# A bucketed attention and expert kernel: denominators of the last pair by one-column products, route and gather steps in the order list, a new order

## The chip, the cores and the metric

The program runs on one core of one Trainium2 chip. The metric is the device time of one execution in microseconds. The kernel before took 443.05 us (median of three runs, 442.56 to 443.46).

## The reference

Attention in which a query sees only the keys of its own hash bucket (six signs of a projection), and then a mixture of eight experts, of which each token goes to one:

```python
mask = q_bucket[:, :, :, None] == k_bucket[:, :, None, :]
scores = scale * np.matmul(q, k.transpose(0, 1, 3, 2))
scores = np.where(mask, scores, -1000000000.0)
attn = np.exp(scores - np.max(scores, axis=-1, keepdims=True))
attn = attn / (np.sum(attn, axis=-1, keepdims=True) + 1e-09)
x = np.matmul(attn, v)                       # B, H, S, D = 2, 8, 768, 64
...
# x as [B, S, 512]; per batch, in the order of the tokens s:
e = fresh_e if s == 0 or local_gate[b, s] < 0.5 else prev_e   # fresh_e = argmax(logits)
h = np.maximum(x[b, s] @ w1[e], 0.0)         # w1: 8, 512, 1024
out[b, s] = p[e] * (h @ w2[e])               # w2: 8, 1024, 512
```

All inputs and outputs are fp32.

## The kernel before

The 16 heads are worked as eight pairs, p = 0 to 7 (four to a batch); the two heads of a pair lie side by side on the partitions or the columns of TensorE. Queries and keys are cut in six tiles of 128 and two halves of 384. Per pair:

- `s1(p, i, kh)`: scores of query tile i against half kh of the keys, two terms (rounded values; bucket bits), and their row maximum on VectorE (line 262).
- `s2(p, kt, half)`: transposed scores of key tile kt against half of the queries, four terms, and the exponential on ScalarE (line 309) into a `pt` tile, of which there are ten.
- `padd(p, kt, h)`: the sums of the `pt` tiles, kept as `SP[p, h]` (line 316), on VectorE or GpSimd as `MOVED` says. `pv` multiplies `pt` by V (line 323), `flat` adds the uniform rows (line 330).
- `hp`, `hd`, `bd`: bucket bits of the next pair; `hi`, `lo`: its split in a rounded value and a rest, on ScalarE, VectorE or GpSimd; `ma`, `mb`, `mc`, `mf`: maxima, transposed and sent by DMA. `lx` loads q and k of a pair.
- `sa`, `sb`: the denominators of a pair, by a product of a ones matrix with `SP`, a copy on ScalarE, and transposes back. The last pair has its own `sah`, `sbh`, by halves: there `SP` holds the sum of the first five (half 0) or four (half 1) `pt` tiles, and further products with ones add the rest (lines 342 to 363).
- `ot`, `ug`: copy of the output, transposes with the gate's product (line 417), normalization into the token rows `XT` and the logits `GR` (lines 425, 430).

`route(b, halves)` is a generator that chooses the expert and the slot of each token and scatters the rows to DRAM `xs` (line 555). It runs on VectorE, with transposes on TensorE, and stops at each `yield`; `step()` runs it to the next one. There are three: batch 0, and the two halves of batch 1. The first expert's tokens of batch 1 don't take the way through DRAM: they are gathered by products with one-hot matrices (`onehot`, lines 635 and 712) on top of the batch 0 rows that `xa` read back (line 751). `we`, `wh`, `wl` and `ve` load and split the first expert's weights. `ready` splits the gathered rows, and `hidden(0, ...)` begins the experts (line 735). `busy` are idle products at the start.

The order of all of it, up to the last `ugh`, is the list `ORDER`: each word is a step, issued in this order to every engine's and queue's own in-order stream. `MOVED` chooses the engine or the queue of a step (0 or 1). Score buffers, and all others in PSUM of the tag `big`, are three of two banks each. After the list some steps stand in the code (gather, `late` normalization, last route steps).

Of the kernel before, what the change touches and what calls it, by code (L numbers as in the profile page):

```python
# [6 lines left out]
F32 = mybir.dt.float32  # L7
F32R = mybir.dt.float32r
# [52 lines left out]
padd.5.4.0 padd.6.1.0 s2.6.2.0 s2.6.3.1 s1.7.1.0 s1.7.1.1 pv.5.4.1 pv.5.5.1 padd.5.5.1 padd.5.5.0 pv.5.5.0 s1.7.2.0
s1.7.2.1 ot.5 s1.7.3.0 mf.6 we.0 we.1 we.2 we.3 pv.6.0.1 pv.6.0.0 s2.6.1.1 s1.7.3.1 s2.6.3.0 s2.6.2.1 lo.7.1 padd.6.1.1 s1.7.4.0 s2.6.4.1
step s2.6.4.0 s2.6.5.1 wh.0 wh.1 s1.7.4.1 padd.6.2.1 pv.6.1.1 pv.6.1.0 s1.7.5.0 padd.6.2.0 s1.7.5.1 sa.5 pv.6.2.1 pv.6.3.1
pv.6.2.0 padd.6.3.0 pv.6.4.1 pv.6.3.0 ma.7 flat.6.0 mb.7 sb.5 ug.4 ug.5 mc.7 step padd.6.3.1 split_h.0 flat.6.1
s2.7.2.0 s2.6.5.0 split_h.1 pv.6.5.1 padd.6.4.0 pv.6.4.0 pv.6.5.0 ot.6 padd.6.4.1 padd.6.5.1 wl.0 wl.1 s2.7.1.0 s2.7.0.0
s2.7.5.0 s2.7.3.0 s2.7.1.1 padd.6.5.0 s2.7.4.0 step padd.7.1.0 mf.7 we.4 we.5 ve.0 ve.1 ve.2 ve.3 split_l.0 s2.7.0.1 sa.6 padd.7.2.0 pv.7.0.0 padd.7.3.0
pv.7.1.0 padd.7.4.0 split_l.1 step wh.2 wh.3 wh.4 pv.7.2.0 sb.6 ug.6 wh.5 wl.2 wl.3 wl.4 wl.5 flat.7.0 padd.7.1.1 sah.7.0 pv.7.3.0 pv.7.4.0 pv.7.5.0 sbh.7.0
oth.7.0 ugh.7.0 s2.7.2.1 s2.7.3.1 step pv.7.0.1 padd.7.2.1 flat.7.1 xa.0 step s2.7.5.1 split_h.2 s2.7.4.1 padd.7.3.1
pv.7.1.1 pv.7.2.1 xa.1 step step hle.0 pv.7.3.1 hle.1 ohe pv.7.4.1 sah.7.1 pv.7.5.1 oth.7.1 sbh.7.1 ugh.7.1
step  # L70
# [7 lines left out]
    "padd": {(0, 3, 1): 1, (1, 1, 0): 1, (1, 1, 1): 1, (1, 2, 0): 1, (1, 2, 1): 1, (1, 3, 1): 1, (1, 5, 1): 1, (2, 1, 1): 1, (2, 2, 0): 1, (2, 2, 1): 1, (2, 5, 0): 1, (2, 5, 1): 1, (3, 5, 0): 1, (4, 1, 1): 1, (4, 2, 1): 1, (4, 3, 0): 1, (4, 4, 0): 1, (5, 1, 0): 1, (5, 2, 0): 1, (6, 1, 0): 1, (6, 1, 1): 1, (6, 2, 1): 1, (6, 5, 0): 1, (7, 1, 0): 1, (7, 1, 1): 1, (7, 2, 0): 1, (7, 2, 1): 1, (7, 3, 0): 1, (7, 3, 1): 1, (7, 4, 0): 1},  # L78
    "split_l": {(2,): 1, (3,): 1},
    "wl": {(2,): 1, (3,): 1, (4,): 1, (5,): 1},  # L80
}

# [44 lines left out]
def tile_kernel(ctx, tc, qT, kT, v, proj, wg, w1, w2, cst, out):  # L127
# [210 lines left out]
    def sah(p, half):  # L338
        st = ps.tile([128, 2, 512], F32, tag="big", name="st")
        ST[p, half] = st  # L340
        for h in range(2):
            nc.tensor.matmul(out=st[32 * h:32 * h + 32, 0, 0:384], lhsT=ones, start=True, stop=False,
                             rhs=SP[p, half][:, h * 384:h * 384 + 384], tile_position=(0, 32 * h))
        for kt in range(5 - half, 6):
            for h in range(2):
                nc.tensor.matmul(out=st[32 * h:32 * h + 32, 0, 0:384], lhsT=ones, start=False, stop=(kt == 5),
                                 rhs=PT[p, kt, half][:, h * 384:h * 384 + 384], tile_position=(0, 32 * h))
        ss = smp.tile([64, 384], F32, tag="ss", name="ss", bufs=1)
        nc.scalar.activation(out=ss, in_=st[0:64, 0, 0:384], func=ACTF.Copy)
        NF[p] = ss  # L350
# [594 lines left out]
```

## Time and profile before

| | us |
|---|---|
| median of three runs | 443.05 |
| the profiled execution, its own time | 442.57 |
| its span, first to last instruction | 440.8 |
| TensorE busy in the span | 424.1 |
| VectorE busy | 285.5 |
| ScalarE busy | 211.2 |
| GpSimd busy | 171.8 |

TensorE's busy time counts pipelined products, whose ends are modelled, so products overlap in it; the distances between their starts tell what each costs. The granted clock of TensorE was 0.995 of full speed over the span. In the views below PE is TensorE, PEld its weight load, DVE VectorE, ACT ScalarE, POOL GpSimd and SP the queue of SyncE; a line number is one of the kernel before.

### The profile page before, as it was taken

Reading aid. Unit: us, or ns where it says so; the run is one execution under the profiler, and the core shown is the slowest. Engines: PE = TensorE matmul, PEld = TensorE weight load, DVE = VectorE, ACT = ScalarE, POOL = GpSimd, SP = SyncE. Lnnn points to the kernel's source line nnn. Section 1 sums busy time; section 2 is a strip of 40 time slices with the busy share of each in tenths; the row PEclk is TensorE's granted clock in tenths of the full one; section 3 lists DMA queues with packets and bytes.
Section 4 is the critical chain, followed back from the end, with each engine's and each line's share of the span. In section 5 each row is a group of like instructions: output and inputs, shape, how many; then the busy total and the mean of one; then the engine's idle time right before and its main releaser. Section 6 shows DMA issues by size and latency. Waiting matters only on the chain.

```text
span 440.8 us, 8126 instructions
## 1 busy us (share of the span) xinstructions
PE 424.1 (96%) x3208; PEld 327.0 (74%) x3208; DVE 285.5 (65%) x453; ACT 211.2 (48%) x290; POOL 171.8 (39%) x124
## 2 busy tenths in 40 slices
PE   8899999999999999999999899999999999999993
PEld 6655575847667566766665898989898989898993
DVE  6766887678466677686988775967565646474110
ACT  3534372716536345362744255757564646463110
POOL 6595545546878636959153121010000000000001
PEclk9999999999999999999999999999999999999998
DMA  7212341224062100310353199997767676750000
GB/s 269 93 41 78 74 141 45 68 76 133 26 217 103 37 13 6 110 38 2 97 193 114 20 268 369 337 328 263 259 201 272 194 268 216 245 165 2 38 2 32
DMA packets 42612, 60.08 MB, mean 136 GB/s; under 512 B 5431, under 2 KB 25129, under 8 KB 42572
## 3 DMA queue, kind: packets, MB, share of 16 engines
q1 hardware_dynamic: 39081, 50.15, 35.5%
q0 software_dynamic: 2432, 6.84, 4.2%
q10 hardware_dynamic: 1059, 2.56, 1.7%
q8 instruction: 26, 0.43, 0.4%
q14 instruction: 14, 0.11, 0.1%
HBM read 47.75 MB, written 11.56 MB: 135 GB/s over the span
## 4 chain that ended last, share of the span: by engine, by line
issue 41%; PE 39%; POOL 6%; DVE 6%; DMA 4%; ACT 0%; POOLq 0%; SPq 0%; DVEq 0%
PE s L253 21%; PE pv L323 13%; POOL out L855 4%; PE ug L417 2%; DVE mx L262 2%; POOL xs L555 2%; DVE sp L316 2%; DMA xk<-kT 2%; PE st L375 1%; DMA xq<-qT 1%; PE pv L330 1%; DVE rE L514 1%; DMA xs<-xt,rsi 1%; PE hb L192 1%; DMA xa<-xs 1%
## 5 line engine op out<-in xcount | busy, mean ns | idle before, releaser
L262 DVE TENSOR_REDUCE mx<-s 128x2 f32<-128x768 f32 x96 | 88.8, 954 | 33.6 <-PE s L253 32.8
L309 ACT ACTIVATE pt<-s 128x768 f32<-128x768 f32 x96 | 74.7, 810 | 47.9 <-PE s L253 46.3
L802 DVE TENSOR_TENSOR wl<-st,wh 128x1024 fp32r<-128x1024 f32 x56 | 67.1, 1221 | 46.7 <-ACT wh L801 46.2
L316 POOL TENSOR_TENSOR sp<-sp,pt 128x768 f32<-128x768 f32 x40 | 75.0, 1887 | 44.4 <-DVE sp L316 35.3
L253 PE MATMUL s<-hx 64*128 64x384 f32 x384 | 72.7, 374 | 2.8 <-DVE mx L262 2.5
L801 ACT ACTIVATE wh<-st 128x1024 fp32r<-128x1024 f32 x56 | 58.3, 1057 | 26.2 <-DMA st<-w 13.3
L323 PE MATMUL pv<-pt,v 128*64 128x384 f32 x384 | 69.9, 496 | 0.0
L855 POOL DMA_INDIRECT out<-y,xsl x13 | 13.2, 1013 | 140.2 <-ACT y L848 140.2
L253 PE MATMUL s<-b,b 64*128 64x384 f32 x372 | 63.0, 334 | 0.0
L253 PEld LDWEIGHTS s<-hx 64*128 64x128 f32 x384 | 36.0, 183 | 27.9 <-DVE mx L262 7.7
L735 PE MATMUL hps<-xH,wh 128*128 128x256 f32 x224 | 53.8, 276 | 0.0
L735 PE MATMUL hps<-xH,wl 128*128 128x256 f32 x224 | 53.7, 277 | 0.0
L845 PE MATMUL yps<-wh,hH 128*128 128x512 f32 (+1 forms) x136 | 52.2, 383 | 0.0
L845 PE MATMUL yps<-wh,hL 128*128 128x512 f32 (+1 forms) x136 | 51.6, 380 | 0.0
L845 PE MATMUL yps<-wl,hH 128*128 128x512 f32 (+1 forms) x136 | 51.4, 378 | 0.0
L323 PEld LDWEIGHTS pv<-pt,v 128*64 128x64 f32 x384 | 24.4, 136 | 31.9 <-issue 31.0
L735 PEld LDWEIGHTS hps<-xH,wl 128*128 128x128 f32 x224 | 42.1, 188 | 0.3
L735 PEld LDWEIGHTS hps<-xH,wh 128*128 128x128 f32 x224 | 42.1, 188 | 0.3
L738 DVE SCALAR_TENSOR_TENSOR hL<-hps,hH 128x512 fp32r<-128x512 f32 x32 | 22.0, 686 | 22.2 <-ACT hH L737 22.2
L253 PEld LDWEIGHTS s<-b,b 64*128 64x128 f32 x372 | 35.1, 184 | 0.0
L735 PE MATMUL hps<-xL,wh 128*128 128x256 f32 x224 | 34.5, 276 | 0.0
L253 PE MATMUL s<-hx,lx 64*128 64x384 f32 x192 | 32.5, 333 | 0.0
(211 smaller groups left out, 631.5 us busy)
## 6 DMA issues: line engine op xcount, KB each, us to landing
st<-w SPq DMA_DIRECT2D x56, 512.0 KB
xs<-z SPq DMA_DIRECT2D x8, 513.0 KB
st<-w SPq DMA_DIRECT2D x13, 256.0 KB
xsl<-xs SPq DMA_DIRECT2D x6, 514.0 KB
v<-v SPq DMA_DIRECT2D x12, 256.0 KB
xq<-qT SPq DMA_DIRECT2D x6, 384.0 KB
xk<-kT ACTq DMA_DIRECT2D x4, 384.0 KB
xk<-kT SPq DMA_DIRECT2D x4, 384.0 KB
```

The costliest lines, as they stand in the source:

```text
L253: nc.tensor.matmul(out=sc[:, h, 0:384], lhsT=w[r, cols[0]], rhs=x[r, cols[1]], tile_position=(64 * h, 0), start=first and n == 0, stop=las ...
L262: nc.vector.tensor_reduce(out=MX[p][:, kh, i // 3, :, i % 3], in_=sc[:, :, 0:384], axis=AX.X, op=ALU.max)
L309: nc.scalar.activation(out=pt.rearrange("p (a q) -> p a q", a=2), in_=sc[:, :, 0:384], func=ACTF.Exp, scale=0.125)
L316: eng.tensor_tensor(out=SP[p, h], in0=PT[p, 0, h] if kt == 1 else SP[p, h], in1=PT[p, kt, h], op=ALU.add)
L323: nc.tensor.matmul(out=PV[p][64 * h:64 * h + 64, half, 0:384], lhsT=V[b, kt][:, pp * 128 + 64 * h:pp * 128 + 64 * h + 64], rhs=PT[p, kt, h ...
L417: nc.tensor.matmul(out=t[:, half, j * 146:j * 146 + 146], lhsT=OT[p][:, q * 128:q * 128 + 128], rhs=iw[:, pp])
L735: nc.tensor.matmul(out=hps[:, k], lhsT=w, rhs=x, start=(k, n) in ends[0], stop=(k, n) in ends[1])
L738: LAST["DVE"] = nc.vector.scalar_tensor_tensor(out=hL, in0=hps, scalar=0.0, in1=hH.bitcast(F32), op0=ALU.max, op1=ALU.subtract).ins
L801: nc.scalar.activation(out=H, in_=st, func=ACTF.Copy)
L802: nc.vector.tensor_tensor(out=L, in0=st, in1=H.bitcast(F32), op=ALU.subtract)
L845: nc.tensor.matmul(out=yps[:, us], lhsT=h[:, k, ts], rhs=w[:, k, us], start=(n == 0), stop=(n == 23))
L855: i = nc.gpsimd.indirect_dma_start(out=dst, out_offset=bass.IndirectOffsetOnAxis(ap=idx, axis=0), in_=y[:, us], in_offset=None, bounds_che ...
```

## The change

Three things change. The denominators of the last pair become products with one column of ones: `SP` is the stationary operand, cut in 128 columns, so that the sums come out with the queries on the partitions, and no copy and no transposes follow. For that `SP` must hold all six `pt` tiles: three `padd` are new (7.5.0, 7.4.1, 7.5.1). The steps that stood behind the list are now words of it (`rows`, `ge`, `gl`, `oh`, `late`, `ready`), and `step` names its generator and runs one piece. And the whole list and most of `MOVED` are new.

```diff
 MOVED = {
-    "bd": {(4, 0, 0): 1, (5, 0, 1): 1, (5, 1, 1): 1, (7, 0, 1): 1, (7, 1, 0): 1},
-    "hi": {(0, 1): 1, (7, 0): 1, (7, 1): 1},
...
-    "split_l": {(2,): 1, (3,): 1},
-    "wl": {(2,): 1, (3,): 1, (4,): 1, (5,): 1},
+    "hi": {(3, 1): 1, (4, 1): 1, (5, 0): 1},
+    "hle": {(1,): 1},
+    "lo": {(0, 0): 1, (0, 1): 1, (1, 0): 1, (1, 1): 1, (2, 0): 1, (3, 1): 1, (4, 0): 1, (4, 1): 1, (5, 1): 1, (6, 0): 1, (7, 0): 1, (7, 1): 1},
+    "lx": {(1, 1): 1, (2, 0): 1, (4, 0): 1, (5, 1): 1, (7, 0): 1},
...
+    "split_l": {(0,): 1, (1,): 1, (2,): 1, (3,): 1},
+    "wl": {(0,): 1, (1,): 1, (2,): 1, (3,): 1, (4,): 1, (5,): 1},
 }
+LEFT = {0: (), 1: ()}
...
     def sah(p, half):
         st = ps.tile([128, 2, 512], F32, tag="big", name="st")
         ST[p, half] = st
+        terms = [SP[p, half]] + [PT[p, kt, half] for kt in LEFT[half]]
         for h in range(2):
-            nc.tensor.matmul(out=st[32 * h:32 * h + 32, 0, 0:384], lhsT=ones, start=True, stop=False,
-                             rhs=SP[p, half][:, h * 384:h * 384 + 384], tile_position=(0, 32 * h))
-        for kt in range(5 - half, 6):
...
-        ss = smp.tile([64, 384], F32, tag="ss", name="ss", bufs=1)
-        nc.scalar.activation(out=ss, in_=st[0:64, 0, 0:384], func=ACTF.Copy)
+            for j in range(3):
+                for n, x in enumerate(terms):
+                    nc.tensor.matmul(out=st[:, 0, 3 * h + j:3 * h + j + 1], lhsT=x[:, h * 384 + 128 * j:h * 384 + 128 * j + 128],
+                                     rhs=ones[:, 0:1], start=(n == 0), stop=(n == len(terms) - 1))
 
     def sbh(p, half):
-        for j in range(3):
-            nc.tensor.transpose(st[:, 1, j * 64:j * 64 + 64], ss[:, j * 128:j * 128 + 128], idf[0:64, 0:64])
...
-    def step():
-        while RT and next(RT[0], True):
-            RT.pop(0)
+    def step(i):
+        next(RT[i], None)
...
-        nc.vector.tensor_tensor(
+        (nc.vector, nc.gpsimd)[moved("hle", i)].tensor_tensor(
             out=hl[1], in0=XT[1][:, 0:3, c], in1=hl[0].bitcast(F32), op=ALU.subtract)
```

The list begins and ends like this now; what stood behind it is gone from the code, up to the last route step:

```
busy.2 lx.0.0 busy.2 clear lh0 busy.2 lcs busy.2 lx.0.1 lhw ident dh.0.0 dv.0.0 dh.1.0 hi.0.1 dh.1.1 dv.1.0 hi.0.0
dv.1.1 da.0.0 da.1.0 s1.0.0.0 da.1.1 s1.0.1.0 lo.0.0 busy.2 busy.2 load_v.0.4 s1.0.2.0 busy.2 dh.0.1 dv.0.1 s1.0.0.1
load_v.0.0 lx.1.1 hi.1.1 busy.2 da.0.1 lx.1.0 s1.0.1.1 s1.0.2.1 busy.2 busy.2 hp.1 hi.1.0 md.0 load_v.0.1 ma.0.0
...
padd.7.4.0 s2.7.1.1 s2.7.5.0 s2.7.0.1 sa.6 pv.7.0.0 flat.7.0 wl.2 step.0 split_l.0 we.5 split_l.1 padd.7.5.0 step.0
sb.6 wh.5 ug.6 xa.0 pv.7.2.0 pv.7.1.0 padd.7.1.1 padd.7.2.1 pv.7.4.0 pv.7.3.0 pv.7.5.0 sah.7.0 wl.1 oth.7.0 sbh.7.0
ugh.7.0 step.1 s2.7.3.1 s2.7.4.1 padd.7.3.1 padd.7.4.1 s2.7.5.1 xa.1 step.1 pv.7.0.1 flat.7.1 pv.7.2.1 padd.7.5.1
pv.7.4.1 pv.7.1.1 split_h.2 pv.7.3.1 step.1 pv.7.5.1 sah.7.1 wh.4 step.1 sbh.7.1 ohe oth.7.1 ugh.7.1 late step.2
rows.2 hle.0 split_h.3 split_l.2 rows.0 rows.1 hle.1 step.2 split_l.3 ge.0 rows.3 ge.1 ve.3 ge.2 step.2 oh step.2 wl.5
wl.4 ve.2 ge.3 gl.0 gl.1 ready.0 gl.2 gl.3 ready.1
```

## Rows read from the trace of the kernel before

**Rows 1.** Windows B, C, D: busy us (instructions) by engine, clock, DMA, GB/s

```profile
16.60:202.20 185.60, 182.62 (x1532) 118.78 (x1532) 132.18 (x201) 87.08 (x122) 120.18 (x75) 1.00 0.24 72
202.20:250.40 48.20, 45.36 (x357) 31.52 (x355) 42.10 (x116) 22.80 (x40) 18.63 (x15) 1.00 0.28 94
250.40:440.80 190.40, 182.32 (x1232) 166.82 (x1232) 100.63 (x117) 94.69 (x119) 22.47 (x22) 0.99 0.61 201
```

**Rows 2.** Timeline, TensorE, a visit to pv: start us, us, line, operation, operands

```profile
187.91 0.34 PE L253 MATMUL s<-b,b 64*128 64x384 f32 x2
188.18 1.51 PE L323 MATMUL pv<-pt,v 128*64 128x384 f32 x8
189.62 0.44 PE L253 MATMUL s<-hx 64*128 64x384 f32 x2
```

**Rows 3.** Chain of waits in order of time, a long run of pv: start, us, what

```profile
198.63 3.38 PE pv L323 x20
```

**Rows 4.** Timeline, TensorE, score blocks that wait for a buffer

```profile
48.26 0.33 PE L253 MATMUL s<-hx 64*128 64x384 f32 x2
48.43 0.34 PE L253 MATMUL s<-b,b 64*128 64x384 f32 x2
49.13 0.44 PE L253 MATMUL s<-hx 64*128 64x384 f32 x2 [0.36 <-DVE mx L262]
49.41 0.34 PE L253 MATMUL s<-b,b 64*128 64x384 f32 x2
```

**Rows 5.** Waits of the score weights' load: us in total, times, longest

```profile
PEld s L253 <- DVE mx L262: 7.7, 17, 1.1
...
PEld s L253 <- ACT pt L309: 6.4, 25, 0.9
```

**Rows 6.** Timeline of the start, ScalarE and VectorE

```profile
5.41 0.84 ACT L235 ACTIVATE hx<-xq 128x768 fp32r<-128x768 f32 x1 [2.73 <-DMA xq<-qT]
6.85 2.35 DVE L211 TENSOR_SCALAR bt<-hb,cs 128x384 f32<-128x384 f32 x4
7.49 1.72 ACT L216 ACTIVATE b<-bt,cs 128x384 fp32r<-128x384 f32 x3 [1.24 <-DVE bt L211]
```

**Rows 7.** Groups by line: busy us, mean ns of one, idle before

```profile
L262 DVE TENSOR_REDUCE mx<-s 128x2 f32<-128x768 f32 x96 | 88.8, 954 | 33.6 <-PE s L253 32.8
...
L316 DVE TENSOR_TENSOR sp<-sp,pt 128x768 f32<-128x768 f32 x21 | 23.1, 1102 | 0.2
...
L316 POOL TENSOR_TENSOR sp<-sp,pt 128x768 f32<-128x768 f32 x40 | 75.0, 1887 | 44.4 <-DVE sp L316 35.3 <-ACT pt L309 5.1 <-PE s L253 3.0
```

**Rows 8.** Timeline, an add on GpSimd beside one on VectorE

```profile
104.35 2.12 POOL L316 TENSOR_TENSOR sp<-pt 128x768 f32<-128x768 f32 x1 [0.39 <-ACT pt L309]
104.70 2.59 DVE L316 TENSOR_TENSOR sp<-sp,pt 128x768 f32<-128x768 f32 x1
...
108.22 0.44 PE L253 MATMUL s<-hx 64*128 64x384 f32 x2 [0.78 <-DVE mx L262]
```

**Rows 9.** Timeline of window C, TensorE's small products

```profile
233.61 0.33 PE L523 MATMUL tb<-cs,rC 8*128 8x8 f32 x3
...
238.16 0.39 PE L355 MATMUL st<-cs,ss 64*128 64x64 f32 x3
...
239.67 1.05 PE L751 MATMUL xt<-cs,xa 128*128 128x128 f32 x8
```

**Rows 10.** Timeline of window C, VectorE, and the first hidden product

```profile
237.74 0.95 DVE L650 TENSOR_TENSOR xhl<-xt,xhl 128x768 fp32r<-128x768 f32 x1
238.60 0.87 DVE L635 TENSOR_SCALAR oh<-io,RK 128x256 fp32r<-128x256 f32 x3
...
241.64 0.55 DVE L425 TENSOR_TENSOR xt<-ug,r 128x384 f32<-128x384 f32 x1
...
248.88 1.48 DVE L757 TENSOR_TENSOR x0L<-xt,x0H 128x512 fp32r<-128x512 f32 x2
...
250.41 0.38 PE L735 MATMUL hps<-x0H,b 128*128 128x256 f32 x1 [1.41 <-DVE x0L L757]
```

More of the change, by code (lines that the diff above doesn't have):

```diff
@@ L65 @@
[L65 to L68, printed above, removed]
@@ L69 @@
[L69 to L70 removed]
+busy.2 lx.0.0 busy.2 clear lh0 busy.2 lcs busy.2 lx.0.1 lhw ident dh.0.0 dv.0.0 dh.1.0 hi.0.1 dh.1.1 dv.1.0 hi.0.0
+dv.1.1 da.0.0 da.1.0 s1.0.0.0 da.1.1 s1.0.1.0 lo.0.0 busy.2 busy.2 load_v.0.4 s1.0.2.0 busy.2 dh.0.1 dv.0.1 s1.0.0.1
+load_v.0.0 lx.1.1 hi.1.1 busy.2 da.0.1 lx.1.0 s1.0.1.1 s1.0.2.1 busy.2 busy.2 hp.1 hi.1.0 md.0 load_v.0.1 ma.0.0
+lx.2.0 busy.2 lo.1.1 s1.0.3.0 md.1 hd.1 lo.0.1 load_v.0.3 mb.0.0 s1.0.4.0 s2.0.5.0 s1.0.5.0 s2.0.0.0 load_v.0.5
@@ L704, in first_w @@
         return [t[:, 128 * o:128 * o + 128] for t in (WH[k], WL[k])]
-    parts = {f.__name__: f for f in (
-        bd, busy, clear, da, dh, dv, fill_slots, fill_some, flat, hd, hi, hle, hp, ident, io, iwl, lcs, lhw, lo, load_v, lh0, lx, md,
-        ma, mb, mc, mf, ohe, ot, oth, padd, pv, s1, s2, sa, sah, sb, sbh, split_h, split_l, step, ug, ugh, ve, vsum, we, wh, wl, xa)}
-    def gather(oh, hl, c0, c1, last=False):
-        for c in range(c0, c1):
-            for j in range(3):
-                for k in range(2):
-                    nc.tensor.matmul(out=xt0[c // 2][:, c % 2], lhsT=hl(k, j, c), rhs=oh[:, j], start=False,
-                                     stop=(last and c % 2 == 1 and j == 2 and k == 1))
@@ L715, in early, with rows @@
-    def early(k, j, c):
-        return HLE[c // 2][k][:, j, 128 * (c % 2):128 * (c % 2) + 128]
+    xt0, X0, OH = {}, {}, []
+    def rows(c):
+        if c % 2 == 0:
+            pool, tag = ((pvp, "pv"), (ps, "big"))[c // 2]
+            xt0[c // 2] = pool.tile([128, 2, 512], F32, tag=tag, name="xt0")[:, 0].rearrange("p (c n) -> p c n", c=2)
+        for t in range(2):
+            nc.tensor.matmul(out=xt0[c // 2][:, c % 2, 128 * t:128 * t + 128], lhsT=XA[t][:, 128 * c:128 * c + 128], rhs=idf,
+                             start=(c % 2 == 0 and t == 0), stop=False)
@@ new lines, in gather, with ge, gl, oh @@
+    def gather(oh, c, hl, last=False):
+        for j in range(3):
+            for k in range(2):
+                nc.tensor.matmul(out=xt0[c // 2][:, c % 2], lhsT=hl(k, j), rhs=oh[:, j], start=False,
+                                 stop=(last and c % 2 == 1 and j == 2 and k == 1))
+    def ge(c):
+        gather(OHE[0], c, lambda k, j: HLE[c // 2][k][:, j, 128 * (c % 2):128 * (c % 2) + 128])
+    def gl(c):
+        gather(OH[0], c, lambda k, j: XHL[k][:, j, 128 * c:128 * c + 128], True)
+    def oh():
+        OH.append(onehot("oh", 3))
@@ new lines, in late, with ready @@
+    def late():
+        LATE.pop()()
+    def ready(i):
+        h, l = (vp.tile([128, 576], F32R, tag="v", name=n)[:, 48:560].rearrange("p (c n) -> p c n", c=2) for n in ("x0H", "x0L"))
+        nc.scalar.activation(out=h, in_=xt0[i], func=ACTF.Copy)
+        nc.vector.tensor_tensor(out=l, in0=xt0[i], in1=h.bitcast(F32), op=ALU.subtract)
+        X0[i] = h, l
+    parts = {f.__name__: f for f in (
+        bd, busy, clear, da, dh, dv, fill_slots, fill_some, flat, ge, gl, hd, hi, hle, hp, ident, io, iwl, late, lcs, lhw, lo, load_v, lh0, lx, md,
+        ma, mb, mc, mf, oh, ohe, ot, oth, padd, pv, ready, rows, s1, s2, sa, sah, sb, sbh, split_h, split_l, step, ug, ugh, ve, vsum, we, wh, wl, xa)}
@@ L781, in tile_kernel @@
         ph = ctx.enter_context(tc.tile_pool(name="ph", bufs=4, space=PSUM, reuse_waits="tile"))
-        step()
+        for i in (1, 2):
+            step(i)
         nc.gpsimd.dma_start(out=PI, in_=xs[0:CAP, 512:514].rearrange("(t p) c -> p t c", p=128))
```

123 lines of the change are left out of this document (43 added, 80 removed), and 2 rows, old and new, of the table MOVED.

## The prediction

> **What bounds the kernel now.** I read the windows first, cut at the first score block that is exponentiated (16.6), the transposes of the last pair's maxima (202.2) and the first product of the first expert (250.4). I call the stretches A, B, C, D. In B TensorE is busy 182.6 of 185.6 us and in D 182.3 of 190.4, at full clock, with VectorE at 132 and 95. C is different: TensorE 45.4 and VectorE 42.1 of 48.2 us [rows 1]. The chain of waits agrees: score and pv products up to 207 us, then almost only VectorE and the scatters of the route. The change rewrites A to C; D keeps its code.
>
> Then TensorE's timeline, for what a place in the order costs. Score slots (two products side by side) start 0.17 us apart [rows 4]; a pv block takes 0.65, since five blocks last 3.38 and two 1.44 [rows 2, 3]. A visit to pv has a price: the score slot before it lasts 0.27 instead of 0.17, two blocks last 1.44 instead of 1.30 [rows 2], and the first score slot behind lasts 0.28 instead of 0.17 [rows 4]. Part of the 0.14 belongs to the change of half inside pv, so I put a visit at 0.30 us.
>
> Then what is left idle in B. Eight score blocks start over 0.5 us after the slot before; one stands in [rows 4], 0.70 behind, waiting for VectorE's maximum to free a score buffer. The eight gaps sum to 5.5 us, of which 8 x 0.17 is work: 4.1, and 0.9 more for their slow first slots (0.11 each). The waits view has 42 waits of the score weights' load for VectorE or ScalarE [rows 5]; the other 34, at 0.11, give 3.7. So some 8.7 us of B are waits for score buffers; the rest is TensorE's own work.
>
> **The change part by part.** *A.* The first kT leaves the head of ScalarE's queue and is issued on SP behind qT, hw0 and the constants; its rounding moves from VectorE to ScalarE, in front of the other one (0.84 each) [rows 6]. An estimate: kT there at 5.7 (both had landed by 5.41), two roundings and two of the da copies (1.72 / 3 = 0.57 each) end at 8.5, and the first score block comes 0.2 us later than now. VectorE then has its six maxima, but one of the four dv (2.35 / 4 = 0.59) falls between them; all four now end before the first [rows 6]. Sum +0.8; I take +0.9 (bounds 0 and 1.5, the latter if lx.1.1, now issued behind da.1.1 on ScalarE, holds up hp.1). Two more s1 fit into that wait, so B is rid of them.
>
> *B, work.* I counted both orders up to the last mb. The new one leaves one s2 (4 slots, 0.7), three pv (0.65 each) and a flat (0.2, half a pv block and less) more for C: -2.85. Two s1 went to A: 2 x 0.35 = -0.7. But scores are entered 41 times instead of 30: 11 x 0.30 = +3.3. *B, waits.* A score buffer comes free when the block three allocations earlier has been read: 0.95 for a maximum [rows 7], a little less for an exponential, and some 0.15 of handing over (an estimate from the start of VectorE's step behind TensorE's last slot). Counting TensorE's work between the two, the order now falls short at 15 places, by 2.6 us together, most of it between 30 and 52 us, where six s1 stand in a row; the new one at 6 places, by 0.4 us. If the 8.7 us shrink in that ratio, 1.3 stay and 7.4 go. The count sees no queue on VectorE or GpSimd, so I take 5.0 off, with bounds 1 and 7.4.
>
> Behind that, adds on VectorE before the last mb fall from 22 to 14 (1.10 us each now) [rows 7], so maxima are reached sooner. GpSimd has eight adds more in B, 8 x 1.89 = 15.1, and two lo fewer, -3.6: busy 131.7 of about 180 instead of 120.2 of 185.6 [rows 1, 7]. I cost that at 0, hidden as long as no exponential waits for a buffer that the sums still read; the first rival prices that.
>
> One row speaks against loading GpSimd. At 104.70 an add on VectorE took 2.59 us while GpSimd's add ran from 104.35 to 106.47; the maximum behind it came late, and TensorE sat 0.78 us at 108.22 [rows 8]. The Trainium skill, page "SBUF — State Buffer", section "SBUF: two separate sides", has the rule: the port pair shared by VectorE and GpSimd is an exclusive lock held for a whole instruction, and the other engine blocks. The trace agrees here: the add ended 0.82 behind GpSimd's. By the rows, VectorE's two-input operations in B go from 24 (22 adds, 2 lo) to 20 (14 adds, 4 lo, 2 wl) while GpSimd's busy share goes from 0.65 to 0.73: 15.6 meetings against 14.6. So 0 in the sum; the bad case is in the first rival.
>
> *C.* Denominators of the last pair: now 10 slots of half a pv block (0.33), two copies on ScalarE and twice three transposes (0.39) [rows 9], 4.1 us of TensorE. Then: 24 products of one column. The trace shows none. The nearest rows are the 8-column transposes behind a 128-column load, 0.11 each at most (three in 0.33), and fp32 products of 128 x 128 by 128, 0.13 at most (8 in 1.05) [rows 9]: 2.6 to 3.1 at most; I take 2.6, the narrower one being nearer. But TensorE isn't late here: the last transposes ended at 238.55, and VectorE was at the one-hot until 239.47, ahead of the denominators in its queue [rows 9, 10]. So the shorter route gains 0; at best the two copies, some 0.6 each.
>
> VectorE pays instead. Behind the last mb it has four adds more (the three new ones and 6.5.1), 4 x 0.95 = 3.8, and split_l.0 and .1 from GpSimd, about half of an hle subtraction each, 1.0; hle.1 (0.95) leaves it [rows 10]. 42.1 + 3.9 = 46.0 us of work. If today's 6.1 us of idle stay, C lasts 52.1; if they cover it all, 48.2. By place: up to the last logits one add more and two hle fewer, -1.0. Behind them `late` (0.55, until now in the shade of the transposes before the scans), hle.0 (0.95) and split_l.2 (0.5) stand before the last scans, less some 0.6 of that shade: +1.4. wl.5 and wl.4 (a third and the whole of an add's length) stand before x0L, and the first hidden product started when x0L had ended (250.36, 250.41) [rows 10]: +1.4. That is +1.8; one s2 and three pv more lie under VectorE. I take +2.5, bounds 0 and 3.9. The route's scatters keep their distance: from the end of the first batch's arithmetic to xa's landing it took 14 us, and rows.2 has 15 us of TensorE's work in between. ve.2 and ve.3 are issued last on SP, behind xa.1; they are wanted in the second hidden block, so I leave D at 0.
>
> **The sum.** A +0.9; B -2.85 - 0.7 + 3.3 - 5.0 = -5.25; C +2.5; D 0: -1.85. The profiled execution took 442.57 (span 440.8, 1.8 around it), so 440.7; the median of the runs shown is 0.5 above it: 441.2.
>
> **The rivals.** (1) *The sums hold up the exponentials; slower.* There are ten pt buffers. If freed ones are reused in the order in which they came free, five s2 of the new order (2.1.5.1, 2.4.5.1, 2.4.3.1, 2.6.3.1, 2.2.1.0) take one whose last reader, an add on GpSimd, stands one to three places ahead; now the closest is six ahead. From the point where GpSimd is a whole add behind, each holds ScalarE for up to 1.89 us, of which two free score buffers cover about 1.0: 5 x 0.9 = 4.5. Blocked adds as at 104.70 do the same. With 1 us of waits saved: 0.9 - 1.25 + 4.5 + 2.5 = +6.7, 450; with half of the 4.5 and 3 saved +2.4, 445.5. For it: GpSimd at 73%. Against: adds become ready long before their place. Chance 0.13.
> (2) *VectorE sets the whole of C; slower.* C +3.9 and 3 saved: 0.9 - 3.25 + 3.9 = +1.5, 444.6. For it: VectorE is at 87% there already. Against: 6.1 us of idle. Chance 0.16.
> (3) *Nothing to measure.* C +3.9 with 5 saved, or C +2.5 with 3 or 4: -0.9 to +0.2, so 442.2 to 443.2. Chance 0.20.
> (4) *The order does all that it can.* 7.4 saved and C +1: -5.8, 437.3. Chance 0.13.
>
> **How the numbers follow.** My forecast, 0.9 to 4 us faster (439 to 442.1), has 0.38; its time is 441.2. The range, 437.3 to 446.0, leaves out the upper half of (1) and the lower part of (4). Faster by over 0.2% (0.9 us, about what a measurement of this kernel can tell from no change): 0.38 + 0.13 = 0.51; within: 0.20; slower: 0.29.
>
> **What would show it.** In the changed kernel: the first exponentiated block at 17.4 to 17.6; the last mb's transposes near 198 (at 202 or later, the waits were not saved); fewer score-load waits than 42; from those transposes to the first hidden product 50 to 52 us with VectorE busy some 46 of them; the denominators behind VectorE's queue, not TensorE's. Exponentials that wait for GpSimd's sums would show rival (1). If C is shorter than 48 us, I misread which engine sets it.

## The result, and the profile after

The changed kernel took 438.18 us (median of four, 436.97 to 439.37) beside 443.18 for the kernel before: ratio 0.9889, 95% interval 0.9855 to 0.9922. Timed again in the experiments it had 0.9926 (0.9907 to 0.9945). So it is 0.7 to 1.1% faster, 3.3 to 5.0 us; I had forecast 1.85 us and called 437.3 the best case.

The profiled execution took 437.44 us, its span 435.6. The windows of its stages, cut at the same landmarks as [rows 1], with A ahead (columns as there):

```profile
0.00:18.03 18.03, 15.00 (x98) 9.90 (x99) 10.86 (x22) 7.28 (x12) 8.99 (x14) 1.00 0.64 207
18.03:194.10 176.07, 175.70 (x1505) 116.90 (x1504) 130.48 (x196) 82.37 (x119) 126.23 (x79) 1.00 0.26 76
194.10:244.32 50.22, 47.24 (x380) 34.99 (x376) 41.94 (x118) 21.14 (x37) 17.83 (x13) 1.00 0.27 93
244.32:435.60 191.28, 182.48 (x1234) 166.76 (x1232) 102.92 (x120) 96.30 (x121) 22.57 (x22) 0.99 0.60 200
```

A +1.4, B -9.5, C +2.0, D +0.9 in the profiled execution. In B TensorE is busy 175.7 of 176.1 us: nothing is left to take out of B but TensorE's own work. The waits view answers [rows 5]:

```profile
PEld s L259 <- DVE mx L268: 6.3, 13, 0.6
PEld s L259 <- ACT pt L315: 5.5, 13, 0.6
```

26 waits instead of 42, and none over 0.6 us. The idle us of a weight load are no idle us of TensorE, which works meanwhile; the count and the longest are what to read.

C and D, from TensorE's timeline (start, us): the first hidden product, which no longer waits for x0L as it did in [rows 10], and the next expert's transposes, which now wait for their rows.

```profile
244.20 0.28 PE L714 MATMUL xt<-oh,xl 128*128 128x256 f32 x1
244.32 1.60 PE L756 MATMUL hps<-x0H,b 128*128 128x256 f32 x12
...
265.05 1.09 PE L804 MATMUL xps<-cs,xsl 128*128 128x128 f32 x8 [1.25 <-DMA xsl<-xs]
```

### The profile page after: what moved, and what is told of

It is laid out like the page before. It is cut to its first block, busy times and chain, and to the rows that moved or that the text cites. A ratio compares the mean times of both kernels' runs of the same rounds, so it can differ in the third digit from the quotient of the medians.

```text
span 435.6 us, 8104 instructions
## 1 busy us (share of the span) xinstructions
PE 420.4 (97%) x3206; PEld 328.6 (75%) x3206; DVE 286.2 (66%) x454; ACT 207.1 (48%) x288; POOL 175.6 (40%) x126
## 4 chain that ended last, share of the span: by engine, by line
PE 49%; issue 40%; POOL 5%; DVE 1%; DMA 1%; ACT 1%; POOLq 0%; SPq 0%
PE s L259 25%; PE pv L329 15%; POOL out L847 4%; PE ug L414 3%; PE st L372 1%; PE hb L198 1%; POOL xs L551 1%; DMA xk<-kT 1%; PE pv L336 1%; PE st L381 1%; PE busy L605 1%; PE vt L584 0%; POOL xhl L646 0%; DMA PI<-xs 0%; PE st L351 0%
## 5 line engine op out<-in xcount | busy, mean ns | idle before, releaser
L315 ACT ACTIVATE pt<-s 128x768 f32<-128x768 f32 x96 | 71.6, 813 | 52.5 <-PE s L259 52.4
L322 POOL TENSOR_TENSOR sp<-sp,pt 128x768 f32<-128x768 f32 x44 | 82.1, 1877 | 26.9 <-DVE sp L322 20.2
L259 PE MATMUL s<-hx 64*128 64x384 f32 x384 | 71.1, 365 | 0.5 <-DVE mx L268 0.3
L756 PE MATMUL hps<-xH,wh 128*128 128x256 f32 x224 | 53.8, 277 | 0.0
L756 PE MATMUL hps<-xH,wl 128*128 128x256 f32 x224 | 53.8, 277 | 0.0
L759 DVE SCALAR_TENSOR_TENSOR hL<-hps,hH 128x512 fp32r<-128x512 f32 x32 | 22.0, 687 | 19.3 <-ACT hH L758 19.3
```

What stands on the lines that cost most here:

```text
L259: nc.tensor.matmul(out=sc[:, h, 0:384], lhsT=w[r, cols[0]], rhs=x[r, cols[1]], tile_position=(64 * h, 0), start=first and n == 0, stop=las ...
L315: nc.scalar.activation(out=pt.rearrange("p (a q) -> p a q", a=2), in_=sc[:, :, 0:384], func=ACTF.Exp, scale=0.125)
L322: eng.tensor_tensor(out=SP[p, h], in0=PT[p, 0, h] if kt == 1 else SP[p, h], in1=PT[p, kt, h], op=ALU.add)
L756: nc.tensor.matmul(out=hps[:, k], lhsT=w, rhs=x, start=(k, n) in ends[0], stop=(k, n) in ends[1])
L759: LAST["DVE"] = nc.vector.scalar_tensor_tensor(out=hL, in0=hps, scalar=0.0, in1=hH.bitcast(F32), op0=ALU.max, op1=ALU.subtract).ins
```

## The experiments

Stages by TensorE's timeline, in us: A to the first transposes of maxima (mb.0.0), B from there to the last pair's (mb.7), C from there to the first hidden product, then to the next expert's transposes. Beside them the median and the ratio to the kernel before, which ran on the same chip in each group (442.2 to 443.5).

| kernel | A | B | C | to transposes | median | ratio (95%) |
|---|---|---|---|---|---|---|
| before | 16.5 | 185.7 | 48.2 | 19.3 | 443.2 | |
| changed | 17.4 | 176.7 | 50.2 | 20.7 | 438.2 | 0.9889 (0.9855-0.9922) |
| e5 changed again | 18.3 | 176.7 | 50.7 | 19.6 | 438.7 | 0.9926 (0.9907-0.9945) |
| e1 bank | 17.8 | 176.6 | 54.5 | 19.3 | 440.9 | 0.9964 (0.9949-0.9980) |
| e2 wl on GpSimd | 17.9 | 176.7 | 53.8 | 19.6 | 440.8 | 0.9953 (0.9934-0.9972) |
| e3 matrix form | 18.0 | 176.7 | 52.0 | 19.6 | 439.3 | 0.9929 (0.9912-0.9946) |
| e4 no new sums | 18.3 | 176.6 | 55.6 | 19.7 | 443.9 | 1.0018 (1.0001-1.0036) |
| e6 route first | 18.3 | 176.6 | 50.7 | 20.1 | 437.8 | 0.9891 (0.9871-0.9910) |
| e7 idle products | 17.3 | 176.5 | 50.3 | 19.7 | 437.7 | 0.9906 (0.9883-0.9928) |
| e8 old engines | 20.7 | 183.8 | 50.4 | 19.6 | 446.4 | 1.0079 (1.0053-1.0104) |
| e9 old order, new engines | 16.6 | 201.3 | 48.1 | 19.3 | 458.5 | 1.0348 (1.0324-1.0373) |
| e10 rows of six | 18.3 | 186.1 | 50.3 | 19.3 | 448.7 | 1.0134 (1.0109-1.0159) |
| e11 first key | 16.6 | 176.5 | 50.7 | 20.5 | 436.9 | 0.9865 (0.9844-0.9887) |
| e12 combined | 18.4 | 176.7 | 50.8 | 19.6 | 437.5 | 0.9885 (0.9866-0.9905) |

B repeats within 0.2 us wherever order and engines are the same. Where the last part of the list is the changed kernel's, C lies at 50.2 to 50.8. A varies by up to 3.4 us, with the first key's landing and with the moment at which TensorE reached its full clock: from the first rounding of kT to the first transposes of maxima it takes 11.1 us in the six profiles of this start whose clock record begins by 6.1 us, and 11.5 to 12.9 in the four where it begins at 9.7 to 13.7 (last section).

### What made B shorter: e8, e9, e10

e8 gives the sums of pairs 0 to 6 their old engines in the new order (its edit is shown); e9 is the reverse, the new engines in the old order:

```diff
-    "padd": {(0, 1, 1): 1, (0, 4, 1): 1, (1, 3, 0): 1, ...
+    "padd": {(0, 3, 1): 1, (1, 1, 0): 1, (1, 1, 1): 1, ...
```

> The changed kernel with the sums of pairs 0 to 6 on the engines of before (22 of them on VectorE up to the last mb instead of 14). It tells apart what saved the waits for score buffers in B (9.5 us off B, of which 8.0 are gaps between score products). Theory (the order of the scores and pv products): B grows by 0 to 2. Rival (VectorE's shorter queue, since maxima are reached sooner): B grows by 4 to 6. Second rival (GpSimd's sums hold up exponentials in the changed kernel): B shrinks.

> The kernel before, with the sums of pairs 0 to 6 on the changed kernel's engines (14 of them on VectorE up to the last mb instead of 22, eight more on GpSimd); its order stays. With the old engines in the new order, B grew by 7.2 of the 9.5 us (stretches between the pairs' mb transposes), because maxima came late. Theory A (fewer adds on VectorE save the waits in any order): B 4 to 7 us shorter than 185.6, the execution 4 to 7 faster than before. Theory B (order and engines are a pair: an add helps or hurts by what stands behind it in its engine's queue): B between 2 shorter and 5 longer than before.

e8: B 7.1 longer, so the rival held, and by more than its 4 to 6: most of B's gain is lost if VectorE has 21 adds up to the last mb (the trace's count; I had counted 22) instead of 14. TensorE waits for maxima whose turn comes late. One place is the transposes of one pair's maxima, behind two adds and a subtraction on VectorE. The widest, 2.10 us, has another cause beside one add of VectorE: the route's short two-input operations ahead of the maximum, 0.2 us each in the changed kernel, took 1.5 to 1.8 beside adds of GpSimd (timeline of e8):

```profile
69.95 1.81 DVE L322 TENSOR_TENSOR sp<-sp,pt 128x768 f32<-128x768 f32 x2
71.69 0.95 DVE L268 TENSOR_REDUCE mx<-s 128x2 f32<-128x768 f32 x1
72.56 1.98 DVE L251 TENSOR_TENSOR lx<-xq,hx 128x768 fp32r<-128x768 f32 x1
...
75.14 0.22 PE L291 MATMUL tp<-idr,nf 128*24 128x128 f32 x1 [1.73 <-DVE f L284]
...
166.26 5.57 POOL L322 TENSOR_TENSOR sp<-sp,pt 128x768 f32<-128x768 f32 x3 [0.89 <-DVE sp L322]
...
168.17 1.82 DVE L491 SCALAR_TENSOR_TENSOR rf<-rw,cs 128x48 f32<-128x48 f32 x1
...
170.14 1.76 DVE L493 TENSOR_TENSOR rw<-req,rf 128x48 f32<-128x48 f32 x1
...
175.47 0.44 PE L259 MATMUL s<-hx 64*128 64x384 f32 x2 [2.10 <-DVE mx L268]
```

But fewer adds on VectorE are no gain in themselves. e9 has as few, and its B is 15.6 longer than before, three times theory B's bound. Eight adds more stand in GpSimd's queue, ahead of work that TensorE waits for (the sum of V, at 147). And where six of them run one behind the other, from 202.68 to 213.49, VectorE's short two-input route operations, 0.2 us each alone, take 1.5 to 1.8 here too, so that a maximum behind them is late, its score buffer comes free late, and TensorE waits 4.11 for it with a pair's denominators (at 211). The timeline of e9:

```profile
140.40 1.30 POOL L584 TENSOR_TENSOR va<-v 128x512 f32<-128x512 f32 x1
141.78 5.30 POOL L586 TENSOR_TENSOR va<-va,v 128x512 f32<-128x512 f32 x4
...
147.13 1.22 PE L588 MATMUL vt<-va,ones 128*16 128x512 f32 x2 [4.01 <-POOL va L586]
...
202.68 10.81 POOL L316 TENSOR_TENSOR sp<-sp,pt 128x768 f32<-128x768 f32 x6
...
204.60 1.79 DVE L495 SCALAR_TENSOR_TENSOR rf<-rw,cs 128x48 f32<-128x48 f32 x1
...
206.54 1.73 DVE L497 TENSOR_TENSOR rw<-req,rf 128x48 f32<-128x48 f32 x1
...
211.05 1.51 PE L375 MATMUL st<-sp,ones 128*32 128x384 f32 x8 [4.11 <-DVE mx L262]
```

Not all of the 15.6 is these waits. In or behind each of its three widest holes e9's granted clock fell to 0.50, for 3.4, 3.4 and 6.8 us (windows of e9, clock third from the end). Half of what TensorE worked in these stretches, up to 6 us by an estimate from these lengths, is the lower clock's price:

```profile
50.00:57.00 7.00, 5.58 (x42) 4.89 (x44) 4.38 (x6) 2.13 (x3) 5.80 (x4) 0.76 0.36 105
147.00:152.00 5.00, 4.87 (x20) 3.64 (x22) 2.86 (x3) 0.63 (x1) 5.00 (x5) 0.66 0.26 79
207.00:217.00 10.00, 5.95 (x26) 2.09 (x28) 6.07 (x10) 0.49 (x1) 10.00 (x6) 0.66 0.01 2
```

So order and engines are a pair. From mb.0.0 to mb.7, the new order with the old engines saves 2.0 us, the new engines in the old order cost 15.6, and both together save 9.1.

e10 leaves the engines and moves 18 words, three at each of the pairs 2 to 7, here at pair 2:

```diff
-s1.2.0.0 s1.2.0.1 s1.2.1.0 ... pv.0.2.1 pv.0.5.0 s2.1.0.1 s1.2.1.1 ... s1.2.3.1 pv.0.5.1 s1.2.3.0
+s1.2.0.0 s1.2.0.1 s1.2.1.0 s1.2.1.1 s1.2.3.1 s1.2.3.0 ... pv.0.2.1 pv.0.5.0 s2.1.0.1 ... pv.0.5.1
```

> The changed kernel with six score blocks whose maxima VectorE reads put in a row at the head of pairs 2 to 7, where the new order has rows of three (18 words moved forward; as many visits to pv, all engines as they are). Theory (the new order's spacing saves the waits for score buffers): in the kernel before such a row at 49 us made four blocks wait by 0.51 to 0.63 each, 2.2 us; six rows give 8 to 13 us more in B. Rival (VectorE is early enough now, so a row costs little): 0 to 3 us more.

B is 9.4 longer, within the theory's 8 to 13: between the pairs' transposes by 1.63, 1.20, 1.71, 1.57, 1.63 and 1.67: 1.57 for a row, less than the 2.2 of the kernel before. The waits are back in the waits view of e10: 30 of the load for VectorE instead of 13, and 19 of the products themselves:

```profile
PEld s L258 <- DVE mx L267: 16.4, 30, 0.7
...
PE s L258 <- DVE mx L267: 5.2, 19, 0.4
```

### What sets C: e1 to e7

e1 puts the last gathered chunks back into the bank in which the kernel before had them, where the first hidden tile follows:

```diff
     def rows(c):
+        held = [ps.tile([128, 2, 512], F32, tag="big", name="skip") for _ in range(c if c == 2 else 0)]
+        for t in held:
+            skip(t)
...
+        for t in held:
+            skip(t)
```

> The changed kernel, with two idle score buffers held (four 8x8 transposes) while the buffer of the last two gathered chunks is allocated, so that this buffer is again the one whose banks the first hidden tile takes over, as in the kernel before. Theory: the forecast for C (+2.5) came out near (+2.0) because two errors cancel. VectorE's last steps did come later as argued, but the first hidden product no longer waits for x0L (it began at 244.32, 0.12 after the last gather product, while x0L ended at 246.3; in the kernel before it began at 250.41 when x0L ended at 250.36). With the bank of before it waits again: first hidden product at 246.3 to 246.5, so C +2.0; the next expert's rows (waited for 1.25 at 265.05) are then there in time, so the execution is 0.5 to 1.0 slower, not 2.0. Rival: the first hidden product is bound by the products before it, whatever the bank: 244.3 to 244.5 and no change.

The wait for x0L came back, 1.93 as expected, and the next expert's transposes wait for nothing. So placement took it away in the changed kernel, where another order of buffers put those chunks elsewhere. The timeline of e1:

```profile
248.96 1.64 PE L764 MATMUL hps<-x0H,b 128*128 128x256 f32 x12 [1.93 <-DVE x0L L740]
```

But C is 3.8 to 4.3 longer and the execution 2.3 to 2.7, not 0.5 to 1.0, and the rest wasn't expected. The edit does more than move the bank: behind its transposes into the held buffers, the products that put the batch 0 rows into the chunks now wait 1.58 for VectorE (at 235.05; in the changed kernel they run from 232.67). And the granted clock falls; what each of the two costs can't be parted here. In these windows of e1 (clock third from the end) TensorE idles 1.7 of 4.5 us, after one-column and other short products, and then runs at its lower level, 1.2 GHz:

```profile
226.24:230.78 4.54, 4.54 (x31) 2.06 (x30) 3.99 (x9) 1.16 (x3) 1.33 (x1) 1.00 0.28 107
230.78:235.32 4.54, 2.82 (x21) 2.44 (x21) 3.95 (x22) 1.67 (x4) 0.78 (x1) 0.89 0.80 231
235.32:239.87 4.55, 4.55 (x22) 4.04 (x22) 2.75 (x7) 0.92 (x2) 3.93 (x4) 0.50 0.44 174
```

e2 takes wl.4 and wl.5 off VectorE:

```diff
-    "wl": {(0,): 1, (1,): 1, (2,): 1, (3,): 1, (4,): 1, (5,): 1},
+    "wl": {(0,): 1, (1,): 1, (2,): 1, (3,): 1},
```

> The changed kernel with the last two pieces of the first expert's rest (wl.4, wl.5) on GpSimd, as before, instead of on VectorE. Theory: VectorE's queue carries the chain that ends the route: x0L and the last route steps stand behind wl.4 and wl.5 (1.26 us at 243.90); behind the route come the last three scatters, the read of their rows and the transposes at 265.05, which waited 1.25 for them. So the last route step comes 1.2 earlier (245.6 instead of 246.87), the transposes no longer wait for their rows, and the execution is 1.0 to 1.25 faster (D 190.0 to 190.3 instead of 191.3). Rival: D is bound by the weights' transfers (ScalarE waits 21.7 us for them, 13.3 before), so the time comes back there: no change (within 0.3).

Both were wrong: C is 3 us longer. (The expectation also misnames the kernel before: there wl.4 and wl.5 ran on VectorE too, ahead of the route's last steps.) VectorE's last scan took 4.44 us instead of 2.01, through three GpSimd instructions in a row, and TensorE waited 2.12 for it (timeline of e2):

```profile
237.94 1.75 POOL L646 TENSOR_TENSOR xhl<-xt,xhl 128x768 fp32r<-128x768 f32 x1
...
238.50 4.44 DVE L512 TENSOR_TENSOR_SCAN rC<-rE,rC 8x384 f32<-8x384 f32 x1
...
239.63 2.49 POOL L683 TENSOR_TENSOR w<-st,w 128x256 fp32r<-128x256 f32 x2
...
243.00 0.37 PE L519 MATMUL tb<-cs,rC 8*128 8x8 f32 x3 [2.12 <-DVE rC L512]
```

The scan ended 0.82 behind GpSimd's last; alone such a scan takes 1.00. The Trainium skill, page "SBUF — State Buffer", section "SBUF: two separate sides", states this for a VectorE operation with two SBUF inputs: the engine that comes second blocks until the other's instruction is over. This trace agrees as to the first of the three GpSimd instructions; the scan then stayed blocked through two more that began after it. The clock fell here too (0.77 of full speed from 230.5 to 235.0, 0.70 from 243.9 to 248.4), so not all of the 3 us need be the scan's.

e3 goes back to the matrix form of the denominators, with the new sums and the new order:

```diff
-                    nc.tensor.matmul(out=st[:, 0, 3 * h + j:3 * h + j + 1], lhsT=x[...], rhs=ones[:, 0:1], ...)
+            nc.tensor.matmul(out=st[32 * h:32 * h + 32, 0, 0:384], lhsT=ones, rhs=SP[p, half][...], ...)
+        nc.scalar.activation(out=ss, in_=st[0:64, 0, 0:384], func=ACTF.Copy)
```

> The changed kernel with the old form of the last pair's denominators (products with a matrix of ones, copy on ScalarE, three transposes per half); the order and the new sums stay. Theory: the form of the products gains next to nothing, since the denominators stand behind the route's steps in VectorE's queue in either form: C within 0.5 of 50.2, the execution 0 to 0.5 slower. Rival: the copies and transposes are on the path of both halves, which the new order no longer hides: 0.6 to 1.2 per half, 1.2 to 2.4 slower.

C is 1.3 to 1.8 longer at full clock, beyond the theory's 0.5; the whole doesn't resolve it (0.9929 against 0.9889 and 0.9926). The size is the rival's, the path isn't. The cost isn't on TensorE: the copy `ss` waits in ScalarE's queue for its products, a weight copy and the route's exponential stand behind it, and VectorE waits 1.36 for that, where the changed kernel waits 0.29 (timeline of e3):

```profile
231.93 0.48 ACT L351 ACTIVATE ss<-st 64x384 f32<-64x384 f32 x1 [3.99 <-PE st L348]
232.31 0.83 ACT L684 ACTIVATE w<-st 128x768 fp32r<-128x768 f32 x1
233.05 0.21 ACT L546 ACTIVATE rex<-rex 128x24 f32<-128x24 f32 x1
...
233.29 0.18 DVE L547 TENSOR_REDUCE rse<-rex 128x3 f32<-128x24 f32 x1 [1.36 <-ACT rex L546]
```

e4 drops the three new sums (`LEFT = {0: (5,), 1: (4, 5)}`):

> The changed kernel without the three new sums: SP holds five and four tiles as before, and one-column products add the other three (42 products instead of 24). Theory: VectorE's queue sets C; it loses three adds of 0.95 (2.85), of which some lies in its idle time (8.3 us in C): C 0.5 to 2 shorter, the execution 0.5 to 2 faster. Rival (the purpose of the change): the extra products cost TensorE as much as the adds cost VectorE (18 products at 0.11 to 0.13: 2.0 to 2.3), and TensorE is the bound: 0 to 1 slower.

My theory fell: 5 us slower. VectorE's work in C went down (41.9 to 40.2), and C went up to 55.6, with TensorE busy 53.8 of it. The rival had the right engine and the wrong count: each one-column product of the code stands twice in the trace, so the 24 of the changed kernel became 60, not 42, and took 8.0 us instead of 3.0 (windows of C for these products alone, PE and PEld, of the changed kernel and then of e4):

```profile
194.07:244.32 50.25, 3.00 (x24) 2.83 (x24) 1.00 0.27 93
194.92:250.47 55.55, 7.98 (x60) 7.81 (x60) 0.94 0.25 84
```

The first 24 of e4 start 0.112 us apart at full clock. At that pace 36 more are 4.0 us, so of the 5.0 some 1.0 is the clock, which fell to 0.50 for 6.8 us inside the second run (windows of e4):

```profile
231.95:236.58 4.63, 4.63 (x37) 4.18 (x33) 2.15 (x14) 1.33 (x3) 1.30 (x2) 0.87 0.62 219
236.58:241.21 4.63, 4.63 (x22) 4.63 (x23) 3.11 (x14) 0.80 (x2) 1.62 (x2) 0.50 0.42 163
241.21:245.84 4.63, 4.17 (x31) 3.62 (x30) 4.58 (x5) 0.46 (x1) 2.13 (x1) 0.89 0.00 0
```

All twelve executions of e4 had a mean clock of 0.980 to 0.988, those of the changed kernel 0.990 to 0.997. What the lower clock cost behind these products isn't shown.

e5 repeats the changed kernel, e6 adds one `step.2` ahead of `wl.5`, and e7 puts six idle products into the hole ahead of the last logits' transposes.

> The changed kernel once more, beside the kernels it is compared with. In three of the four experiments so far TensorE's granted clock fell to 0.50 for 3 to 7 us between 232 and 247 us, in C, which cost some 2 to 4 us; in the profile of the changed kernel it stays at 1.00 there, but one of its four executions had a mean clock of 0.991. Theory A (the fall belongs to the changed kernel's own thin places in C and comes in some executions): the executions spread over 437 to 440 and the slow ones have the lower mean clock (0.991 and below against 0.996). Theory B (only the edits bring it): all executions lie at 437 to 438.5 with 0.995 to 0.997.

> The changed kernel with the last steps of the last route (three short operations on VectorE and the scatters they release) issued ahead of wl.5, wl.4 and x0L instead of behind them. Theory: the chain that ends C and the start of D is VectorE's queue up to the last route step, then the scatters, the read of the rows and the next expert's transposes (which waited 1.25 at 265.05). The last route step comes 2.4 earlier (244.5 instead of 246.87), those transposes wait for nothing, and the execution is 0.8 to 1.3 faster than the changed kernel; x0L comes 0.6 later and costs TensorE 0 to 0.5 in the first hidden block. Rival: the weights' transfers bound D, and D takes it back: no change.

> The changed kernel with six idle products (384 columns, about 1 us together) on TensorE in its longest hole of C, ahead of the transposes that wait for the last logits (a hole of 1.43 at 234.4). Theory A (the clock's fall in C comes from what TensorE does around that hole): fewer executions with a fall, so the median is 0.5 to 1.5 below that of the changed kernel. Theory B (the fall is decided elsewhere, by the 1.5 us of one-column products and the short products before the hole): no change in the executions' clocks, and 0 to 0.3 slower, since the products fill idle time.

e5: 437.5 to 440.7, mean clocks 0.990 to 0.997. The spread is theory A's, but that the falls belong to the changed kernel's C isn't shown: neither of the two profiles of this kernel has a fall there, the kernel before spreads over the same mean clocks (0.990 to 0.997 in its executions beside the experiments), and the slowest execution had 0.993, so the clock isn't all of the spread. e6: the last route step ends 2.5 earlier than in e5 (245.73, 248.19) and the reads of the scattered rows begin 1.1 earlier (255.45, 256.54); the transposes wait for nothing, but those of e5 didn't either, and x0L, later than the products that read it, costs 0.5 in the first hidden block. The median is 0.8 below e5's, the theory's low end, but the intervals touch. e7: 0.9 below, not resolved, and two of its six executions still had 0.989 and 0.993. Whether idle products help stays open.

### The start, and a combined kernel: e11, e12

The edit of e11:

```diff
-busy.2 lx.0.0 busy.2 clear lh0 busy.2 lcs busy.2 lx.0.1 lhw ident ...
+lx.0.1 busy.2 lx.0.0 busy.2 clear lh0 busy.2 lcs busy.2 lhw ident ...
-    "lx": {(1, 1): 1, (2, 0): 1, (4, 0): 1, (5, 1): 1, (7, 0): 1},
+    "lx": {(0, 1): 1, (1, 1): 1, (2, 0): 1, (4, 0): 1, (5, 1): 1, (7, 0): 1},
```

> The changed kernel with the first kT issued at the head of ScalarE's queue again, as in the kernel before, instead of fourth on SyncE's. In the profiles of the changed order the first rounding of kT began at 6.2 to 7.8 us (5.7 was my estimate; 4.40 in the kernel before), and the first mb's transposes followed 1 to 4 us later than before. Theory: kT lands by 4.4 to 5.4, A is 0.6 to 1.5 shorter than in the changed kernel, and as much is saved in the whole. Rival: VectorE's queue (a threshold between the maxima) sets A, so that it stays within 0.3.

The theory held: A 16.6 (17.3 to 18.3 in the others with the key on SyncE, but for e8's 20.7), 436.9 us, which is 1.3 and 1.8 below the two measurements of the changed kernel, and an interval that lies below e5's, though not below the first measurement's. kT's rounding starts at 4.88 instead of 6.31, with the clock up before it in both (timeline of e11):

```profile
4.88 0.84 ACT L240 ACTIVATE hx<-xk 128x768 fp32r<-128x768 f32 x1 [2.22 <-DMA xk<-kT]
```

> The changed kernel with the first kT at the head of ScalarE's queue (A 1.5 to 1.65 shorter in the experiment on it alone), the fourth threshold (dv.0.1) ahead of the first maxima instead of between them, the last route steps and their scatters ahead of x0L, and wl.5 and wl.4 behind x0L instead of ahead of it. Theory: A another 0.3 shorter (six maxima follow each other from 8.7), B as it was (stretches between the pairs' mb transposes within 0.1), C 50 to 51, and the first hidden product to the next expert's transposes 19.3 to 19.7, with neither a wait for the rows (0.9 to 1.25) nor for x0L (0.5): 1.8 to 2.8 faster than the changed kernel, ratio to the kernel before 0.984 to 0.987. Rival: the weights' transfers or a fall of TensorE's clock in C take the last 0.5 to 1 back: as the experiment with the first kT alone, 0.9865.

e12 isn't better than e11 (437.5; its fastest execution, 435.1, is the fastest of all). The path to the transposes is free of both waits, 19.6 as expected. A isn't: the bucket products ran at half the pace up to 9.5 us in the profiled execution, where the clock record begins only at 9.86 (4.14 in e11), and A is 18.4. So e11 has the lowest ratio shown, 0.9865 (0.9844 to 0.9887) of the kernel before; its interval is clear of e5's and overlaps those of e6, e12 and the first measurement.

## Why the prediction was right or wrong

| term | forecast (bounds) | measured |
|---|---|---|
| A | +0.9 (0 to 1.5) | +1.4 |
| B, less work | -3.55 | -4.0 |
| B, visits | +3.3 | +3.9 |
| B, waits | -5.0 (-7.4 to -1) | -9.4 |
| C | +2.5 (0 to 3.9) | +2.0 |
| D | 0 | +0.9 |
| sum | -1.85 | -5.2 |

B is taken apart by the starts of all its products. Work: 16 score products fewer at 0.087, twelve of pv at 0.151, and 0.8 of flat and the sum of V. Visits: score to pv 28 times instead of 19 and to other products 8 instead of 5, 0.18 more than between scores; pv to score 23 instead of 18, 0.27 more than within pv, but pv to others 0.8 less; eleven first slots at 0.11. The waits are what is left of -9.5; the gaps between score products alone give -9.2.

**Bounds and stages.** That TensorE's work bounds B held. That VectorE's queue sets C held only in part: TensorE waits 1.43 for it ahead of the last logits, but e4, with 1.7 us less of VectorE's work and 5.0 more of TensorE's, was 5.3 longer, so TensorE is hardly behind it. B's work and its visits were right within 0.6 each. The direction was right; the gain was about two to three times the forecast (3.3 to 5.0 against 1.85).

**The failed term** is the size of the waits saved. I saw 8.7 us of them, counted that 7.4 would go, and took 5.0, because the count sees no queue on VectorE or GpSimd. 9.4 went, all that I had seen and a little more. The doubt was in the right place with the wrong sign: the adds' engines suit the order, and with the old ones 7.1 us come back (e8). The move of the adds I had costed at 0, with a first rival in which GpSimd's sums hold up exponentials. One exponential did wait 3.5 us for them in e5's profile, and B was no longer for it. As a danger a loaded GpSimd was real: in the old order the same engines cost 15.6, lower clock included (e9). That spacing saves waits is shown from the other side by e10.

**A.** The last of the six maxima ended 0.81 later (15.26 against 14.45), by the late start and the threshold between them, as forecast. Another 0.5: one of the two s1 that I had let fit into the wait stands on the path, ahead of the first exponentiated block (at 18.03, where I had named 17.4 to 17.6 as the sign). And kT was there after my 5.7: its rounding began at 6.2 to 7.8 in the profiles.

**C** came out near its size by errors that cancel. VectorE's work is 41.9, not 46.0. The adds, split_l and hle grew by 3.8 as forecast (11.2, 2.1 and 1.0 us against 7.5, 1.1 and 1.8). But the scans shrank from 10.2 to 8.9: the four subtractions that GpSimd did beside the first four are VectorE's own now (6.3 to 3.9), while the last, beside hle.1 on GpSimd, doubled (1.01 to 2.01). Timelines of the kernel before, then of the changed one:

```profile
206.52 1.83 POOL L687 TENSOR_TENSOR w<-st,w 128x768 fp32r<-128x768 f32 x1
...
206.97 2.19 DVE L514 TENSOR_TENSOR_SCAN rE<-rK,cs 8x384 f32<-8x384 f32 x1
```

```profile
199.23 0.94 DVE L510 TENSOR_TENSOR_SCAN rE<-rK,cs 8x384 f32<-8x384 f32 x1
```

I had used the lock against the change and not for it. And x0L (1.4) and most of wl.4 (0.8) fell behind the boundary; some 0.5 us I can't place. The step "wl.5 and wl.4 stand before x0L: +1.4" failed: they do, but the first hidden product didn't wait for x0L any more (e1). **D** paid for that in the profiled execution: the first hidden product ran ahead of VectorE, whose last route step ended 2.6 us behind its start (246.87, 244.32) where it was 0.5 before (250.87, 250.41). The read of the next expert's rows was issued 2.0 us later behind that start (11.97, 9.95), and it took 8.7 us instead of 4.3, so the transposes waited 1.25. The later route alone doesn't make them wait: in e5, with the same lag, the read took 6.7 us and nothing waited. C and D together: +2.9, against +2.5.

**Denominators.** The 24 products of the trace (12 in the code) took 3.0 us (two runs of 12 in 1.50), within 2.6 to 3.1, above the 2.6 that I took. That they stand behind VectorE's queue held; that the shorter route gains nothing did not quite: without the copy ScalarE's queue is free for the route's exponential, 1.1 us in C (e3).

**The rivals.** The result lies between my forecast's times and rival (4), 0.9 above the latter, though its C +1 was wrong. (2) fell with C and with B, (3) with B.

## What to carry to other kernels

Where two engines feed the bounding one, price the order and the engine of the helpers' work together: one of them alone can be worse than neither. A two-input operation on VectorE's critical chain wants GpSimd's long operations away from it, however short it is itself: a scan of 1.0 us took 4.4 here, and operations of 0.2 took 1.5 to 1.8. So taking work off GpSimd can shorten VectorE. And where a wait ends a stage, look up which bank or buffer the next tile takes over: a new order may remove the wait or bring it back without a line that says so.

## What the runs showed of the hardware that I had not expected

- TensorE's granted clock fell to 0.50 in C in the profiles of e1 (6.8 us), e2 (3.4, twice), e4 (6.8) and e8 (3.4), and in none of the other eight of this order. In e1 it fell in a hole of 1.6 us; in e4 TensorE had not idled, and it fell inside a run of 36 one-column products. C was 3 to 5 us longer in e1, e2 and e4, much of it by other causes; in e8 it wasn't longer (50.4). What decides the fall isn't settled.
- The same four bucket products at the start took 1.56 us in some profiles and 2.93 in others (timelines of the changed kernel and of e8 below), while the clock column showed 1.00 in both. The column is no witness there: the trace's clock record begins only at 6.08 us in the changed kernel and at 13.73 in e8, and where there is no record the column prints 1.00. In all fourteen profiles bucket products ahead of the record's begin start 0.64 to 0.80 us apart and those behind it 0.32 (0.43 the first of a run): a factor of two, as between TensorE's two levels, 1.2 and 2.4 GHz. So by their pace the first products ran at the lower level, for a time that differed from profile to profile (records begin at 4.1 to 13.7 us). Why it differs is open.

```profile
6.33 1.56 PE L212 MATMUL hb<-xk,hw 128*128 128x384 f32 x4 [0.53 <-DMA xk<-kT]
```

```profile
7.82 2.93 PE L212 MATMUL hb<-xk,hw 128*128 128x384 f32 x4 [2.01 <-DMA xk<-kT]
```

- A transfer issued fourth on SyncE's queue, 1.4 us later, was there 1.3 to 2.9 us later (rounding at 6.2 to 7.8 against 4.88) and varied by 1.6 us from one profile to another.
